# Attention with a gated MLP on one core: V straight from DRAM a period ahead, and the value product in three runs with MLP products between

## The chip, the cores and the metric

The kernel runs on one core of one Trainium2 chip. The metric is the device time of one execution in microseconds (us). It was run three times; the profile is of one more execution. TensorE is called PE here, VectorE DVE, ScalarE ACT, GpSimd POOL, and the queue of SyncE, which issues most DMAs, SP.

## The reference, cut to what matters

```python
def _attn_ref(q, k, v):                       # q, k, v: [8, 8, 576, 64] float32
    scores = (1 / sqrt(64)) * q @ k.T
    mask = pos[:, None] // 64 >= pos[None, :] // 64        # causal in blocks of 64
    scores = where(mask, scores, -1e9)
    attn = exp(scores - max(scores))
    attn = attn / (sum(attn) + 1e-9)
    return attn @ v

x = attn_out.transpose(0, 2, 1, 3).reshape(4608, 512)
gate = 1 / (1 + exp(-(x @ w_gate)))           # [512, 1536]
return gate * (x @ w_val) @ w_out             # [1536, 512]
```

The three weights come as 64-bit floats and are converted on the chip.

## The kernel before, in words

**Stages.** The attention takes the first half of the time. It runs over 32 head pairs p (8 batches of 4 pairs). Pairs 0 to 7 are done in one way and pairs 8 to 31 in another (`rest`), which is the one that the change touches. While the attention runs, PE is filled with products of the first third of the MLP (`mlp1`): 144 products of 128 x 512 for each batch, in groups that accumulate in two PSUM banks. The second half of the time is the other two thirds of the MLP (L1123, L1208), which the change leaves alone.

**One period of a late pair.** For pair p, PE computes the scores in three groups (`s`: query blocks 3, 2, and 1 with 0), then those of the last 64 queries of both heads (`t`, the tail). DVE masks them and takes the row maxima (L435, L486). ACT takes the exponentials (L443, L488). DVE then transposes the probabilities in blocks of 32 x 32 into the tile Z (L571 for the blocks, L579 and L582 for the tail). The order on DVE and on ACT is written out by hand (`line`): the tail's transposes come after those of blocks 3 and 2, and those of blocks 1 and 0 after the tail's. Then PE multiplies by V (`z_half`, all through the helper at L308): 144 float32 matmuls on 32 rows and 64 columns of the array, which stand in the trace as 288 records and as many weight loads. It comes in two parts. The first, at step `half`, takes the 10 key blocks that need Z from blocks 3, 2 and the tail (160 records). The second, at step `AV` of the next period, takes the other 8 (128 records). `z_out` (L609, L611) then copies the result, and the next pair's scores follow at once. `FX` multiplies by the reciprocal row sums, which go to DRAM (`r_d`) and come back broadcast (`rb`), splits the result for the MLP and stores it.

**Where MLP products go.** A period is a list of steps with a number of places ("ticks") behind each. For the late pairs the list is `REST`:

```python
REST = (("AV", 0), ("s", 3), ("t", 2), ("tr3", 1), ("tr2", 1), ("trt", 2), ("half", 0), ("trl", 1), ("k", 0), ("FX", 0), ("r", 1), ("q", 1))
```

That is 12 ticks. In each tick `rate` products are put into the order, 3 on the average in the steady state (36 in a period): 9 behind the scores, 18 between the tail's scores and `half`, 9 between the two parts of the value product. The order is held: `half` and `AV` stand behind the last 8 products put before them (`recent`), products put behind them stand behind their last matmul (`hold`), and the scores stand behind the last product. `KEEP` is the number of products that are left when a new batch's products come in.

**V.** One 32-row copy of V is loaded from DRAM for each head (L246, two DMAs of 144 KB), behind the load of the reciprocals on SP. Three more DMAs copy it to the other three groups of 32 partitions (L249, 288 KB each) and wait for the first two. The load for pair p + 1 is put at the end of period p. There are two buffers (`VR`, one of them a part of the tile ZV), so it can start when the value product of pair p - 1 is done. K and Q of pair p + 3 are loaded in steps `k` and `q` (L279, four DMAs each).

**DMA slots.** Every DMA of SP and ACT takes one of eight semaphores in turn, and a DMA waits on its queue until the one that had its semaphore before has landed.

Of the kernel before, what the change touches and what calls it, by code (L numbers as in the profile page):

```python
# [23 lines left out]
KEEP = (52, 32)  # L24
# [8 lines left out]
REST = (("AV", 0), ("s", 3), ("t", 2), ("tr3", 1), ("tr2", 1), ("trt", 2), ("half", 0), ("trl", 1), ("k", 0), ("FX", 0), ("r", 1), ("q", 1))  # L33
# [3 lines left out]
TICKS = 12  # L37
ZB, ZG, ZH = 480, 112, 1920
# [4 lines left out]
def attn_glu_kernel(ctx: ExitStack, tc: tile.TileContext, q, k, v, w_gate, w_val, w_out, out):  # L43
# [142 lines left out]
    with ExitStack() as s2:  # L186
# [53 lines left out]
        def load(p, what, queue=nc.sync):  # L240
            b, hp = pairs[p]
            h0 = 2 * hp
            if what == "v" and p > N_FIRST:
                VR = VRs[(p + 1) % 2]
                for h in range(2):
                    behind(nc.sync.dma_start(out=VR[0:32, h], in_=v[b, h0 + h].rearrange("(t p) d -> p t d", p=32)).ins,  # L246
                           loads["rb"])
                for a in range(1, 4):
                    dma = nc.sync.dma_start(out=VR[32 * a:32 * a + 32], in_=VR[0:32])  # L249
                loads["SP"] = dma.ins  # L250
                return
# [25 lines left out]
            for h in range(2):  # L277
                for j in range(2):
                    bulk(queue.dma_start(  # L279
                        out=r[64 * h + 32 * j:64 * h + 32 * j + 32].rearrange("p (t a) -> p t a", a=32),  # L280
                        in_=src[b, h0 + h, :, 32 * j:32 * j + 32].rearrange("(t p) a -> p t a", p=32)))

        pe_last, first_mm, hold, dealt, chain = [], [], [], [], []
        last, loads, q_copied, recent = {}, {}, [], []

# [21 lines left out]
        def matmul(*args, **kw):  # L307
            pe_last[:] = [nc.tensor.matmul(*args, **kw).ins]  # L308
            in_turn()

        def transpose(*args):
            pe_last[:] = [nc.tensor.transpose(*args).ins]
            if hold:
                behind(pe_last[0], hold[0])
            in_turn()
# [87 lines left out]
        def attend(p):  # L403
# [88 lines left out]
            def recip():  # L492
# [12 lines left out]
                if rest:  # L505
# [5 lines left out]
                    loads["rb"] = dma.ins  # L511
# [3 lines left out]
                loads["rb"] = dma.ins  # L515
# [70 lines left out]
            pv = []  # L586

            def z_half(second):
                if not pv:
                    pv.extend(two_banks() for _ in range(2))  # L590
                VR = VRs[(p + 1) % 2]
                for n, kb in enumerate((0, 4, 1, 5, 2, 6, 3, 7) if second else (8, 12, 9, 13, 10, 14, 11, 15, 16, 17)):
                    g = kb // 4
                    lo, z = (32 * g, ZB * (kb % 4) + (ZG + 32) * g) if g < 4 else (P, 2 * P + 16 * (kb % 4))
                    for a in range(4):
                        at_rows = slice(32 * a, 32 * a + 32)
                        for h in range(2):
                            first = n == 0 and not second
                            matmul(pv[a // 2][rows(h), a % 2, lo:144], lhsT=VR[at_rows, h, kb],
                                   rhs=Z[at_rows, ZH * h + z:ZH * h + z + 144 - lo], start=first,  # L600
                                   stop=(n == (7 if second else 9)), tile_position=(32 * a, 64 * h), skip_group_check=second)
                            if n == a == h == 0:
# [57 lines left out]
            def step(what):  # L660
# [20 lines left out]
                elif what == "half":  # L681
                    z_half(False)
# [8 lines left out]
                elif what == "warm":  # L691
                    if p == 1:
                        warm()
                elif what == "av":
                    if rest:
                        z_half(True)
# [286 lines left out]
        pe_ticks = []  # L983
# [72 lines left out]
        for p in range(n + 1):  # L1056
# [4 lines left out]
            for what, places in (ALONE if p < NP else FIRST if p < N_FIRST else TURN if p == N_FIRST else JOIN if p == N_FIRST + 1 else REST):  # L1061
                if what.startswith(("AV", "TR", "FX")):
                    if prev:
                        prev(what.lower() if what in ("AV", "FX") else what.lower()[:2] + what[2:])
                    if prev and what == "AV" and pairs[p - 1][1] == NP - 1:
# [3 lines left out]
                        rate = (left - KEEP[pb > 0]) / (4 * TICKS)  # L1069
# [7 lines left out]
                elif now:  # L1077
                    now(what)
                for _ in range(places if now else 6 if what == "AV" else 0):
                    pe_ticks.append(pe_last[0])  # L1080
                    acc += rate
                    while acc >= 1:
                        acc -= 1
                        left -= 1
                        ins = next(mlp, None)
# [14 lines left out]
            if N_FIRST <= p and p + 1 < n:  # L1100
                load(p + 1, "v")
# [268 lines left out]
```

## Time and profile before

| | us |
|---|---|
| runs of the kernel before (3): median | 1269.74 |
| lowest, highest | 1256.24, 1270.45 |
| the profiled execution: device time | 1269.53 |
| its span, first to last instruction | 1267.7 |
| PE busy | 1166.6 (92%) |
| DVE busy | 899.1 (71%) |
| ACT busy | 548.3 (43%) |
| POOL busy | 341.6 (27%) |
| mean granted TensorE clock, share of full speed | 0.95 |

A row of a timeline begins with the start and the length in us; "x160" counts the instructions that are merged in it; in brackets stands the idle time before the first of them and what ended it. "issue" means that nothing in the profile held the engine. SPq and ACTq are the queues' own rows. A busy PE is not a PE at full speed: the granted clock (PEclk, as a share) stands beside it.

### The profile page before, as it was taken

To read this page: it belongs to the slowest core of one execution; us is meant where nothing else is said; L and a number is where in the kernel's file an instruction comes from. 1 tells how busy PE (TensorE), PEld (TensorE's weight loads), DVE (VectorE), ACT (ScalarE), POOL (GpSimd) and SP (SyncE) were. 2 spreads that over 40 slices of the span, in tenths; PEclk is the share of its full clock that TensorE was granted. 3 is DMA by queue.
4 is the path that set the end of the run, shared out by engine and by line. 5 is a ranking of instruction groups with operands and counts; after the bars stand their busy time and mean duration, and the time that the engine had idled before them with its cause. 6 is when DMAs were issued, how large, how long until landed. Compare 5 with 4: busy or idle time off the path is not lost.

```text
span 1267.7 us, 30599 instructions
## 1 busy us (share of the span) xinstructions
PE 1166.6 (92%) x12073; PEld 941.5 (74%) x12073; DVE 899.1 (71%) x1844; ACT 548.3 (43%) x1274; POOL 341.6 (27%) x380
## 2 busy tenths in 40 slices
PE   8899789888889878888799999999999999999998
PEld 5566678666767666667577888888888888888887
DVE  5878567556565656565599795888999876768564
ACT  5876435344344434344324444454454532323222
POOL 3446323232231321322230110101111134251402
PEclk9999899888888888888899999999999999999999
DMA  6656555656566556564633314266386956253532
GB/s 162 171 142 152 120 122 116 143 110 144 113 127 137 122 113 136 118 133 111 174 102 109 124 50 133 47 181 164 69 216 242 310 182 211 90 183 104 162 112 72
DMA packets 314688, 175.32 MB, mean 138 GB/s; under 512 B 239152, under 2 KB 279088, under 8 KB 311600
## 3 DMA queue, kind: packets, MB, share of 16 engines
q1 hardware_dynamic: 303744, 154.84, 48.5%
q10 hardware_dynamic: 10416, 17.47, 3.8%
q8 instruction: 95, 1.56, 0.5%
q0 software_dynamic: 384, 1.05, 0.2%
q14 instruction: 49, 0.40, 0.1%
HBM read 104.73 MB, written 47.33 MB: 120 GB/s over the span
## 4 chain that ended last, share of the span: by engine, by line
PE 68%; DMA 11%; DVE 8%; SPq 5%; issue 3%; ACT 3%; POOL 1%; ACTq 0%; DVEq 0%
PE b L1123 26%; PE bank L308 11%; PE m L1208 8%; PE b L1208 8%; PE m L153 8%; PE m L160 4%; DMA VR<-VR 3%; PE bank L153 2%; DMA ZV<-ZV 2%; ACT P L443 2%; SPq L279 2%; DMA r_d<-rT 1%; DMA rb<-r_d 1%; DVE ZV L571 1%; DMA ZV<-in_v_dram 1%
## 5 line engine op out<-in xcount | busy, mean ns | idle before, releaser
L1123 PE MATMUL b<-XH,w 128*128 128x512 f32 (+1 forms) x1120 | 320.9, 368 | 0.8 <-ACT p L1141 0.5
L1123 PEld LDWEIGHTS b<-XH,w 128*128 128x128 f32 x1120 | 203.5, 188 | 37.6 <-ACT p L1141 0.8
L1123 PE MATMUL b<-XL,w 128*128 128x512 f32 (+1 forms) x560 | 205.6, 368 | 0.0
L443 ACT ACTIVATE P<-bank,nm 128x512 f32<-128x512 f32 (+3 forms) x256 | 132.1, 530 | 54.7 <-DVE nm L435 51.7
L1123 PEld LDWEIGHTS b<-XL,w 128*128 128x128 f32 x560 | 105.6, 189 | 17.6 <-DVE XL L958 0.2
L308 PE MATMUL bank<-ZV 32*64 32x48 f32 (+5 forms) x3680 | 83.8, 272 | 24.7 <-DMA ZV<-ZV 14.6
L955 ACT CAST XH<-XB 128x1024 fp32r<-128x1024 f32 (+1 forms) x72 | 66.9, 942 | 88.0 <-DVE XB L953 53.3
L435 DVE TENSOR_REDUCE nm<-bank 128x2 f32<-128x1024 f32 (+3 forms) x128 | 102.5, 821 | 3.1
L308 PEld LDWEIGHTS bank<-ZV 32*64 32x64 f32 (+1 forms) x3680 | 66.9, 142 | 47.7 <-DMA ZV<-ZV 16.9
L609 DVE COPY xT<-bank 128x256 f32<-128x256 f32 x24 | 10.2, 425 | 127.1 <-PE bank L308 127.1
L308 PE MATMUL bank<-ZV,VR 32*64 32x80 f32 (+4 forms) x3456 | 63.5, 275 | 36.6 <-DMA VR<-VR 27.2
L1208 PE MATMUL m<-wo,hH 128*128 128x512 f32 x288 | 93.2, 389 | 0.0
L308 PEld LDWEIGHTS bank<-ZV,VR 32*64 32x64 f32 x3456 | 55.8, 151 | 50.0 <-DMA VR<-VR 25.1
L1208 PE MATMUL b<-wo,hH 128*128 128x512 f32 x288 | 92.9, 389 | 0.0
L160 PE MATMUL m<-wo,hH 128*128 128x512 f32 x256 | 91.3, 427 | 1.6 <-ACT hH L177 1.6
L940 POOL TENSOR_TENSOR XB<-XB 128x256 f32<-128x256 f32 x30 | 23.9, 797 | 248.1 <-DMA XB<-xT_d 190.1
L958 DVE TENSOR_TENSOR XL<-XB,XH 128x1024 fp32r<-128x1024 f32 (+1 forms) x72 | 78.4, 1092 | 13.5 <-ACT XH L955 13.3
L153 PE MATMUL m<-XH,wg 128*128 128x512 f32 x240 | 87.3, 421 | 0.4 <-ACT t L170 0.4
L153 PE MATMUL m<-XH,wv 128*128 128x512 f32 x240 | 86.3, 417 | 0.1
L571 DVE STREAM_TRANSPOSE ZV<-P 128x512 f32<-128x512 f32 (+1 forms) x192 | 80.1, 474 | 0.0
L637 POOL TENSOR_TENSOR xT<-xT,rb 128x576 f32<-128x576 f32 x24 | 34.7, 1448 | 158.1 <-DMA rb<-r_d 53.9
L160 PEld LDWEIGHTS m<-wo,hH 128*128 128x128 f32 x256 | 53.2, 209 | 15.1 <-ACT hH L177 2.9
(214 smaller groups left out, 2467.5 us busy)
## 6 DMA issues: line engine op xcount, KB each, us to landing
XB<-xT_d SPq DMA_DIRECT2D x48, 256.0 KB
prr<-part_d SPq DMA_DIRECT2D x46, 256.0 KB
VR<-VR SPq DMA_DIRECT2D x36, 288.0 KB
ZV<-ZV SPq DMA_DIRECT2D x36, 288.0 KB
part_d<-ost SPq DMA_DIRECT2D x36, 256.0 KB
part_d<-ost ACTq DMA_DIRECT2D x32, 256.0 KB
xT_d<-xT ACTq DMA_DIRECT2D x28, 288.0 KB
rqk<-in_k_dram SPq DMA_DIRECT2D x108, 72.0 KB
```

The costliest lines, as they stand in the source:

```text
L153: mm = nc.tensor.matmul(ps, lhsT=lh, rhs=rh, start=(i == 0), stop=(i == n - 1))
L160: mm = nc.tensor.matmul(ps, lhsT=lh[:, f, t * P:(t + 1) * P], rhs=rh, start=(f == i == 0), stop=(f == F1 - 1 and i == 2))
L279: bulk(queue.dma_start(out=r[64 * h + 32 * j:64 * h + 32 * j + 32].rearrange("p (t a) -> p t a", a=32), in_=src[b, h0 + h, :, 32 * j:32 * ...
L308: pe_last[:] = [nc.tensor.matmul(*args, **kw).ins]
L435: line("DVE", nc.vector.tensor_reduce(out=nm[:, c0:c0 + 2], in_=ps[:, :, c:c + P * (i + 1)], axis=AX.X, op=ALU.max, negate=True), rest)
L443: line("ACT", nc.scalar.activation(out=Pi[:, h], in_=ps[:, h, c:c + n], func=AF.Exp, bias=nm[:, c0 + h:c0 + h + 1], accum_out=sm[:, 5 * h ...
L571: line("DVE", nc.vector.transpose(out=dst[:, :, :4 * ZG].rearrange("p b (g x) -> p b g x", g=4)[:, :, :i + 1, :32], in_=Pi[:, h].rearrange ...
L637: nc.gpsimd.tensor_mul(out=xT, in0=xT, in1=rb)
L955: cut = nc.scalar.copy(out=XO[j][0][:, a:b, c], in_=x)
L958: sub = nc.vector.tensor_sub(out=XO[j][1][:, a:b, c], in0=x, in1=XO[j][0][:, a:b, c].bitcast(F32))
L1123: mm = nc.tensor.matmul(ps, lhsT=lh, rhs=rh, start=(first and k == 0), stop=(k == n - 1), skip_group_check=not first)
L1208: mm = nc.tensor.matmul(po[t], lhsT=lh[:, f, t * P:(t + 1) * P], rhs=rh, start=(half == 0 and i == 0), stop=(half == 1 and i == 5))
```

## The change

V of pair p + 1 is loaded by eight DMAs straight from DRAM, one for each head and group of 32 partitions, at step `tr3` of period p, behind the last marked DMA of SP (`last["SPq"]`, the reciprocals' or the late pairs' K and Q). The value product takes its key blocks in another order (`KBS`) and in two or three runs, whose lengths `av_runs` chooses by a count of issued TensorE instructions. With three runs the next period follows the list `WIDE`: the second run and four ticks come ahead of `AV`. Of the products between the tail's scores and `half`, one tick is moved behind `half`. The rate is worked out again in each period.

```diff
-KEEP = (52, 32)
+KEEP = (52, 40)
-REST = (("AV", 0), ("s", 3), ("t", 2), ("tr3", 1), ("tr2", 1), ("trt", 2), ("half", 0), ("trl", 1), ...
+REST = (("AV", 0), ("s", 3), ("t", 2), ("tr3", 1), ("tr2", 1), ("trt", 1), ("half", 0), ("trl", 2), ...
+WIDE = (("AVa", 4), *REST)
+MEAN = 13.5
+KBS = (8, 12, 9, 13, 10, 14, 11, 16, 15, 0, 4, 1, 5, 2, 6, 3, 17, 7)
+FETCH, FETCH_AT, ROUND, APART, GAP = 256, 192, 32, 25, 24
...
-                for h in range(2):
-                    behind(nc.sync.dma_start(out=VR[0:32, h], in_=v[b, h0 + h].rearrange("(t p) d -> p t d", p=32)).ins,
-                           loads["rb"])
-                for a in range(1, 4):
-                    dma = nc.sync.dma_start(out=VR[32 * a:32 * a + 32], in_=VR[0:32])
+                for a in range(4):
+                    for h in range(2):
+                        dma = nc.sync.dma_start(out=VR[32 * a:32 * a + 32, h],
+                                                in_=v[b, h0 + h].rearrange("(t p) d -> p t d", p=32))
+                        behind(dma.ins, last["SPq"])
+                        last["SPq"] = dma.ins
...
+        def av_runs():
+            x = (FETCH_AT - issued[0]) % FETCH
+            def fits(runs):
+                spans, t = [], 0
+                for r in runs:
+                    spans.append((t, t + ROUND * r))
+                    t += ROUND * r + GAP
+                return all(sum(max(0, min(b, e + FETCH) - max(a, e)) for a, b in spans) <= FETCH - APART
+                           for e in range(x - FETCH, t, FETCH))
+            two = [(n, 18 - n) for n in (9, 10, 8, 11, 7)]
+            three = [(n, m, 18 - n - m) for n in (6, 7, 8, 9, 5, 4) for m in (6, 5, 7, 4, 3)]
+            return next((r for r in two + three if fits(r)), (6, 6, 6))
...
-            def z_half(second):
+            def z_run():
                 if not pv:
                     pv.extend(two_banks() for _ in range(2))
+                    lengths = av_runs()
+                    wide[:] = [len(lengths) > 2]
+                    kbs = list(enumerate(KBS))
+                    runs[:] = [[kbs.pop(0) for _ in range(r)] for r in lengths]
                 VR = VRs[(p + 1) % 2]
-                for n, kb in enumerate((0, 4, 1, 5, 2, 6, 3, 7) if second else (8, 12, 9, 13, 10, 14, 11, 15, 16, 17)):
+                kbs = runs.pop(0)
+                for n, kb in kbs:
...
+            steps = (ALONE if p < NP else FIRST if p < N_FIRST else TURN if p == N_FIRST else JOIN if p == N_FIRST + 1 else
+                     WIDE if wide[0] else REST)
+            ticks = sum(places for _, places in steps)
...
+                    if what == "tr3" and N_FIRST <= p and p + 1 < n:
+                        load(p + 1, "v")
+                new = what == "AV" and pairs[p - 1][1] == NP - 1
+                if p <= N_FIRST and new and p:
+                    rate = (left - KEEP[0]) / (4 * TICKS)
+                elif p > N_FIRST and (new or tick == 0):
+                    i, keep = (p % NP, KEEP[1]) if p % NP or new or p == N_FIRST + 1 else (NP - 1, 0)
+                    rate = max(0, left - keep) / (ticks - tick + (NP - 1 - i) * MEAN)
...
-            if N_FIRST <= p and p + 1 < n:
-                load(p + 1, "v")
```

## Rows read from the trace of the kernel before

**Rows 1.** Windows: late pairs' scores 9 to 31; second half. Length, busy, PEclk, DMA, GB/s.

```profile
core 0: us, PE busy (x) PEld busy (x) DVE busy (x) ACT busy (x) POOL busy (x), PEclk, DMA share, GB/s
146.46:622.34 475.88, 402.00 (x7783) 325.33 (x7778) 282.47 (x683) 197.18 (x575) 134.52 (x177) 0.87 0.58 126
...
660.00:1267.70 607.70, 601.24 (x2801) 502.33 (x2799) 476.46 (x889) 237.71 (x395) 125.82 (x114) 1.00 0.47 144
```

**Rows 2.** Waits of PE over the span: total us, times, longest us.

```profile
PE bank L308 <- DMA VR<-VR: 27.2, 20, 2.3
PE bank L308 <- DMA ZV<-ZV: 14.6, 11, 2.9
PE bank L308 <- issue: 13.8, 8, 4.2
PE bank L308 <- ACT xT L611: 10.3, 3, 4.2
PE m L160 <- POOL hL L178: 4.8, 2, 2.5
```

**Rows 3.** Timeline of PE, one period without a wait: scores, half, products, AV, scores.

```profile
428.44 0.49 PE L308 MATMUL bank<-KH,QH 64*128 64x512 f32 x2
...
437.66 1.99 PE L308 MATMUL bank<-ZV,VR 32*64 32x80 f32 x160
439.58 0.50 PE L153 MATMUL m<-XL,wv 128*128 128x512 f32 x1
...
441.85 2.17 PE L308 MATMUL bank<-ZV,VR 32*64 32x144 f32 x128
443.95 0.50 PE L308 MATMUL bank<-KH,QH 64*128 64x512 f32 x2
```

**Rows 4.** Windows from half to AV: without a wait; with a 1.70 us one; with 1.68.

```profile
437.66:441.92 4.26, 4.26 (x178) 3.58 (x180) 4.19 (x13) 1.76 (x3) 1.50 (x3) 1.00 0.27 68
393.89:402.98 9.09, 7.39 (x177) 5.95 (x180) 4.32 (x13) 2.35 (x4) 3.27 (x6) 0.62 0.68 159
...
479.86:486.31 6.45, 4.72 (x169) 3.72 (x169) 4.31 (x13) 2.35 (x4) 3.29 (x6) 1.00 0.82 203
```

**Rows 5.** Timeline of DVE: tail's transposes in three periods.

```profile
393.14 0.89 DVE L579 STREAM_TRANSPOSE ZV<-Pt 128x128 f32<-128x128 f32 x4 [0.52 <-ACT Pt L488]
...
413.11 0.89 DVE L579 STREAM_TRANSPOSE ZV<-Pt 128x128 f32<-128x128 f32 x4
...
436.79 0.85 DVE L579 STREAM_TRANSPOSE ZV<-Pt 128x128 f32<-128x128 f32 x4
```

**Rows 6.** Timeline of PE: scores that belong to the first two; half of pair 31.

```profile
384.54 0.49 PE L308 MATMUL bank<-KH,QH 64*128 64x512 f32 x2
...
405.02 0.50 PE L308 MATMUL bank<-KH,QH 64*128 64x512 f32 x2
...
634.20 0.40 PE L308 MATMUL bank<-ZV 32*64 32x80 f32 x16 [2.53 <-DVE ZV L579]
634.53 0.59 PE L153 MATMUL bank<-XH,wg 128*128 128x512 f32 x1
```

**Rows 7.** Timeline of PE: a wait of products between half and AV, and the AV after.

```profile
291.90 0.50 PE L160 MATMUL m<-wo,hH 128*128 128x512 f32 x1
...
295.89 0.50 PE L160 MATMUL m<-wo,hL 128*128 128x512 f32 x1 [2.35 <-POOL hL L178]
...
297.90 3.22 PE L308 MATMUL bank<-ZV 32*64 32x144 f32 x128
301.05 0.50 PE L308 MATMUL bank<-KH,QH 64*128 64x512 f32 x2
```

**Rows 8.** Timeline of SP's queue in the period of rows 3.

```profile
426.06 0.98 SPq L246 DMA_DIRECT2D VR<-in_v_dram  x2
430.15 1.99 SPq L249 DMA_DIRECT2D VR<-VR  x3
439.50 2.27 SPq L279 DMA_DIRECT2D rqk<-in_k_dram  x4
```

**Rows 9.** DMA of 426.0:430.15, then 430.15:435.5: packets, MB, share of 16 engines.

```profile
q1 hardware_dynamic: 2553, 0.45, 63.0%
...
q1 hardware_dynamic: 128, 0.88, 79.5%
```

**Rows 10.** Timeline of ACT and its queue around a late store.

```profile
491.21 0.34 ACTq L794 DMA_DIRECT2D part_d<-ost  x1
491.65 0.37 ACT L609 COPY xT<-bank 128x256 f32<-128x256 f32 x1 [5.54 <-DMA rb<-r_d]
```

More of the change, by code (lines that the diff above doesn't have):

```diff
@@ L278, in load @@
                 for j in range(2):
-                    bulk(queue.dma_start(
+                    dma = bulk(queue.dma_start(
                         out=r[64 * h + 32 * j:64 * h + 32 * j + 32].rearrange("p (t a) -> p t a", a=32),
                         in_=src[b, h0 + h, :, 32 * j:32 * j + 32].rearrange("(t p) a -> p t a", p=32)))
+                    if p > N_FIRST + 3:
+                        last["SPq"] = dma.ins
         pe_last, first_mm, hold, dealt, chain = [], [], [], [], []
         last, loads, q_copied, recent = {}, {}, [], []
+        issued = [0]
+        def av_runs():
[10 more added lines that the diff above has]
+            return next((r for r in two + three if fits(r)), (6, 6, 6))
         def mark(engine, ins):
@@ L308, in matmul @@
             pe_last[:] = [nc.tensor.matmul(*args, **kw).ins]
+            issued[0] += 4 if kw["lhsT"].dtype == F32 else 2
             in_turn()
@@ L312, in transpose @@
             pe_last[:] = [nc.tensor.transpose(*args).ins]
+            issued[0] += 2
             if hold:
@@ L510, in recip @@
                                                 in_=tails[:, h].partition_broadcast(D))
-                    loads["rb"] = dma.ins
+                    last["SPq"] = dma.ins
                     return
@@ L514, in recip @@
                     dma = nc.sync.dma_start(out=rb[rows(h), o:o + n], in_=r_f[f:f + n].partition_broadcast(D))
-                loads["rb"] = dma.ins
+                last["SPq"] = dma.ins
                 rb_last[:] = [dma.ins] if p < N_FIRST else []
@@ L597, in z_half @@
                         for h in range(2):
-                            first = n == 0 and not second
                             matmul(pv[a // 2][rows(h), a % 2, lo:144], lhsT=VR[at_rows, h, kb],
-                                   rhs=Z[at_rows, ZH * h + z:ZH * h + z + 144 - lo], start=first,
-                                   stop=(n == (7 if second else 9)), tile_position=(32 * a, 64 * h), skip_group_check=second)
-                            if n == a == h == 0:
+                                   rhs=Z[at_rows, ZH * h + z:ZH * h + z + 144 - lo], start=(n == 0),
+                                   stop=(kb == kbs[-1][1]), tile_position=(32 * a, 64 * h),
+                                   skip_group_check=(kbs[0][0] > 0))
+                            if kb == kbs[0][1] and a == h == 0:
                                 for ins in recent:
@@ L693, in step @@
                         warm()
+                elif what == "ava":
+                    z_run()
                 elif what == "av":
                     if rest:
-                        z_half(True)
+                        z_run()
                         z_out()
@@ L1084, in attn_glu_kernel @@
                         left -= 1
+                        issued[0] += 2
                         ins = next(mlp, None)
```

13 lines of the change are left out of this document (6 added, 7 removed).

## The prediction, made before the changed kernel was run

> **What bounds the kernel now.** First I read the windows of the two halves [rows 1]. In the second half PE is busy for 601.24 of 607.70 us at a granted clock of 1.00, and the change doesn't touch it. From the scores of pair 9 to those of pair 31, 22 periods, PE is idle for 73.9 of 475.88 us and the mean granted clock is 0.87. That stretch is what the change can win in, at 475.88 / 22 = 21.63 us a period. Then I read who PE waited for [rows 2]: V's copies, 27.2 + 14.6 us (VR and ZV are the two buffers), waits that no instruction explains ("issue"), 13.8 us, a copy of ACT, 10.3, and a lower half of the MLP's hidden values from POOL, 4.8. Then I looked for a period without waits, and there is one [rows 3]: scores at 428.44, half at 437.66, products at 439.58, AV at 441.85, the next scores at 443.95. It took 15.51 us. The other 6 us of the mean period are waits and what the clock does after them. The stretch from half to AV shows that best [rows 4]: 4.26 us without a wait, 9.09 with one wait of 1.70 us for V. Of the 4.83 us more only 1.70 are the wait; the other 3.13 are instructions at a lower clock (0.62 granted in the mean; of the two levels, 1.2 and 2.4 GHz, the lower stood for most of it). So a wait of PE is paid about twice or more, when it brings the clock down.
>
> Last I looked at what stands just behind V. In the period without waits the tail's last transposes on DVE run from 436.79 to 437.64 [rows 5], and half starts at 437.66 [rows 3]. From the scores' start to the end of these transposes it takes 9.20 us here, and in two other periods 414.00 - 405.02 = 8.98 and 394.03 - 384.54 = 9.49 [rows 5, 6]. It is a chain of reductions, exponentials and transposes that PE can't shorten, and half needs its end. With 27 products between scores and half, PE arrives at the same moment: the old order is balanced against DVE, and V's lateness hides how tightly.
>
> **The change part by part.**
>
> *V.* Before, two loads are issued from 426.06 and the copies at 430.15 [rows 8], when both have landed; half wants them at 437.66. When the load gets through later they come too late: 31 waits, 41.8 us [rows 2]. After, the load stands a whole period ahead of its use, behind a buffer that is free when AV of the pair before it is done. I take V's waits to go entirely. What it costs on the DMA engines: the three copies took 79.5% of 5.35 us, 4.3 us of 16 engines [rows 9]; the window of the two loads, in which K and Q packets run too, has 2553 small packets at 63% of 4.15 us, or 1.0 us for each 1000. V has 1152 rows of 256 bytes in one copy, so 4608 packets in the new form: 4.7 us against 4.3 + 1.2 = 5.5 before. That is about equal, so with the DMA engines 58% busy [rows 1] I cost it at nothing. On SP's queue eight issues at about 0.49 us (0.98 for two) take 3.9 us instead of 0.98 + 1.99. They stand where SP now waits for the first loads to land, before K's loads at 439.50 [rows 8], a hole of over 7 us after the copies; K, the reciprocals and Q behind them aren't later. The bounds for V are 0 and, if it came as late as now, 41.8 / 22 = 1.9 us a period.
>
> *The runs.* Worked through, `av_runs` never finds two runs: over two runs with a gap of 24 some block of 256 lies inside them and holds 232 or more of their instructions, and 231 are allowed. So it is three runs of about six key blocks, and `WIDE` with 16 ticks, from pair 9 on. Its rate is then near 36 / 16 = 2.25 products a tick (2.5 for a batch's first pair, 1.8 for its last). Between scores and half stand 8 ticks instead of 9, at the lower rate: about 18 products instead of 27. Nine products take 2.27 us (439.58 to 441.85) [rows 3], so PE arrives at half 9.22 - 2.27 = 6.95 us after the scores, while DVE still ends at about 9.2. A new wait of 2.2 us a period takes the place of V's, bounded by 1.5 (20 products, chain 9.0) and 3.1 (14 or 15 products, chain 9.5). It exists already where the last pair's half waited 2.53 us for L579 [rows 6].
>
> From half to the next scores the value product needs 1.92 + 2.10 = 4.02 us as now [rows 3], and two gaps of 9 products, 4.54 us: 8.6 us. A period at full clock is so 9.2 + 8.6 = 17.8 us. This is longer than the 15.51 of the undisturbed period, and shorter than the mean of 21.63.
>
> *The clock.* After a wait of 2.35 us for POOL the next AV took 3.22 us instead of 2.17, and all from 291.90 to 301.05 [rows 7] took 9.15 us where ten products and AV need 4.6 and the waits 2.5 (a short one of ACT among them): some 2.0 us lost. The 1.70 us wait lost 3.13 us; one of 1.68 us lost nothing, its window has a granted clock of 1.00 [rows 4]. So a wait of the new length lowers the clock in some periods and not in others: bounds 0 and 3.1 us a period. I take two of three, at 2.5 us: 1.7 us.
>
> *Instruction stalls.* The "issue" waits stand at L308, the line of the value product and the scores, up to 4.2 us each [rows 2]. With gaps of products in every block of 256 they should mostly go; bounds 0 and 13.8 / 22 = 0.6 us a period, I take 0 here. The Trainium skill says otherwise (Runtime: NRT & Kernel Launch, Instruction fetch mechanics): instructions are refilled in blocks of 256, and the crossing is mostly hidden behind the pace of issue, so that the third run would buy nothing. The trace of before disagrees, with eight such waits of 13.8 us in all; no run here has shown yet that they go with the third run. By that rule, what the waits are would remain, and the sum below would be 1240.
>
> *Other waits.* The copies of ACT and the values from POOL cost (10.3 + 4.8) / 22 = 0.7 us a period now [rows 2]. Some of it falls before half and is covered by DVE's chain: I take 0.2.
>
> The sum is 17.8 + 1.7 + 0.2 = 19.7 us a period, 1.93 less than 21.63; over 22 periods 42.5 us. Against the profiled execution, 1269.5 us with a span of 1267.7 (the median of the runs shown is 1269.74, the same for this purpose), that makes 1227 us. PE's products aren't fewer, only placed differently, so the second half starts that much earlier and takes as long as before.
>
> **The rivals.**
>
> *A, the clock holds.* The wait for DVE stands between products and short runs of six key blocks instead of ten, and the wait of 1.68 us left the clock alone [rows 4]. For it: less light work follows each wait. Against it: 2.35 us brought the clock down [rows 7]. The period is then 17.8 + 0.2 = 18.0 us: 80 us won, 1190.
>
> *B, the clock falls in every period.* The new wait is longer than V's single waits and comes in all 22 periods, V's only in some. The period is 17.8 + 3.1 + 0.4 = 21.3 us, 1262: the gain is given back. For it stand the 3.13 us of [rows 4]; against it the window with 1.00.
>
> *C, slower: ACT held by a store.* ACT works in order, and a store on its queue may have to wait for the DMA that had its slot. At 491.21 a store of a finished part went out only when a load of the reciprocals had landed, and ACT had been idle for 5.54 us [rows 10]; PE's longest wait for such a copy was 4.2 us [rows 2]. Eight V loads in a row take all eight slots. A store placed behind them holds the exponentials, so the chain to half, until V has landed. Such a period costs 19.7 + 4.2 and the rest of the clock's full price, 1.4: 25.3 us. If it strikes in a share x of the periods, the mean is 19.7 + 5.6 x. It breaks even with 21.63 at x = 0.34, and at x = 0.75 the time is 1227 + 22 x 4.2 = 1319. Against it: the loads can go out early in the period, and few waits of that kind show now.
>
> *D, V is late all the same,* because it queues on SP behind K, Q and the reciprocals: 1.9 us of wait beyond DVE's and the rest of the clock's price, 1.4, so 23.0 us and 1300 at worst; half of it, 1263, is likelier. The free buffer and a lead of a whole period speak against it.
>
> **How the numbers follow.** Forecast 0.52 (1205 to 1244), A 0.18, B 0.15, C 0.10, D 0.05. A measurement of this kernel can tell about 2% from no change, that is 1244 to 1295. Faster: forecast and A, 0.70. Same: B and D, 0.20. Slower: C, 0.10. The predicted time is 1227. The range goes from 1187, where A ends, to 1262, which takes in B; it leaves out C, D's worse part and a clock that never falls with a shorter chain.
>
> **What would show it.** If right, the profile after has no wait of PE for V; its new first wait is for DVE's L579 at each half, about 2 us, 20 times or more; the scores' pitch is 19 to 20 us; the granted clock of the stretch is near 0.9; the issue waits have all but gone. The wait for L579 being under 1 us would show my count of products, or the chain's 9.2 us, wrong. A granted clock of 1.00 with 2 us waits would prove A. A wait for ACT or for V's DMA in many periods would prove C or D. If no wait has gone, the forecast is wrong as a whole.

## The result, and the profile after

The changed kernel takes 1215.68 us (median of 4 runs, 1210.44 to 1219.20), the kernel before 1269.17 us beside it. The ratio is 0.9597, with a 95% interval from 0.9525 to 0.9669: faster, by 53.5 us where 42.5 were forecast. The profiled execution took 1219.2 us with a span of 1217.4. In the lines below the old L308 is L332, L571 is L597, L579 is L605, L609 and L611 are L640 and L642, L160 and L178 are L164 and L182, and L246 is L251.

The page's busy times and clock, 40 slices of the span:

```profile
PE 1143.8 (94%) x12073; PEld 914.0 (75%) x12073; DVE 905.3 (74%) x1844; ACT 547.6 (45%) x1274; POOL 340.2 (28%) x380
...
PEclk9999999999989989999899999999999999999999
DMA  7667897897887878796323232545587845344432
```

The waits of PE, as [rows 2]:

```profile
PE bank L332 <- DVE ZV L605: 20.6, 15, 3.7
PE bank L332 <- issue: 20.2, 20, 3.9
PE bank L332 <- ACT t L174: 6.5, 5, 1.3
```

No wait for V is left. In its place stands DVE's L605, the tail's transposes. The five waits named ACT t are the wait of `half` too, and so is the one named ACT Pt (1.6 us). Two of the fifteen lie outside the 22 periods, the 3.7 us one among them. Inside them `half` waits in 19 periods, 0.97 to 1.57 us each, 24.7 us in all and 1.30 in the mean; the first three periods, with 20 to 26 products ahead of `half`, have no such wait over 0.3 us. The third thing to see is the second line: the "issue" waits haven't gone. Their sum is 20.2 us where it was 13.8, but it is a mixed one. Sorted by place (as under "Runs placed by the counted stream"), ten such waits, 13.3 us with one of L164, longest 3.9, are of the kind that made up all eight, 13.8 us, before. One of 2.8 us stands ahead of scores 9, and the others, 0.74 us at most, mostly at the tail's scores and at `half`. So the stalls of the old kind are as large as before.

The windows, as [rows 1]: the 22 periods from scores 9 to scores 31, one of them alone, and the second half:

```profile
148.93:570.43 421.50, 376.85 (x7781) 295.92 (x7777) 283.86 (x683) 195.98 (x574) 133.90 (x177) 0.98 0.83 141
226.05:244.61 18.56, 16.96 (x359) 13.35 (x354) 13.46 (x32) 9.35 (x27) 6.00 (x8) 1.00 0.81 138
660.00:1217.40 557.40, 552.11 (x2587) 462.29 (x2585) 438.36 (x807) 217.18 (x365) 125.68 (x114) 1.00 0.48 148
```

A period takes 421.50 / 22 = 19.16 us instead of 21.63, at a granted clock of 0.98 instead of 0.87. That is 54.4 us over 22 periods. Scores 9 start 2.5 us later than before, and from scores 31 to the end it takes 1.6 us longer (1217.40 - 570.43 against 1267.70 - 622.34): 50.3 us in all between the two profiled executions. The periods had lengths from 15.51 to 26.55 us before; now 20 of 22 lie between 17.4 and 20.2, and two have 23.59 and 24.24.

The timeline of PE for the period of the second window, cut to the scores, the tail's scores, the last product before `half`, the three runs with the products at their ends, and the next scores:

```profile
226.05 0.50 PE L332 MATMUL bank<-KH,QH 64*128 64x512 f32 x2
...
230.13 0.40 PE L332 MATMUL bank<-KH,QBH 128*128 128x288 f32 x1 [0.20 <-ACT P L469]
...
233.57 0.39 PE L157 MATMUL m<-XL,wg 128*128 128x512 f32 x1
235.35 1.34 PE L332 MATMUL bank<-ZV 32*64 32x80 f32 x96 [1.40 <-DVE ZV L605]
236.62 0.73 PE L157 MATMUL m<-XH,wg 128*128 128x512 f32 x2
...
239.11 1.72 PE L332 MATMUL bank<-ZV 32*64 32x80 f32 x96
240.76 0.50 PE L157 MATMUL m<-XH,wv 128*128 128x512 f32 x1
...
243.03 1.65 PE L332 MATMUL bank<-ZV 32*64 32x112 f32 x96
244.61 0.50 PE L332 MATMUL bank<-KH,QH 64*128 64x512 f32 x2
```

Three runs of six key blocks (96 records each), as worked out. On DVE the four transposes that `half` waits for end at 235.49, 9.44 us after the scores' start, where [rows 5, 6] had 8.98 to 9.49; `half` itself starts at 235.35. PE stands ready at 233.96, 7.91 us after the scores' start:

```profile
234.62 0.87 DVE L605 STREAM_TRANSPOSE ZV<-Pt 128x128 f32<-128x128 f32 x4
```

One of the two long periods has this in the timeline of PE: the run that begins at 344.90 stands still for 3.43 us before its last record, and nothing in the profile holds it:

```profile
342.98 0.40 PE L164 MATMUL m<-wo,hH 128*128 128x512 f32 x1
344.90 1.32 PE L332 MATMUL bank<-ZV 32*64 32x80 f32 x95 [1.52 <-DVE ZV L605]
349.65 0.23 PE L332 MATMUL bank<-ZV 32*64 32x48 f32 x1 [3.43 <-issue]
```

### The profile page after: what moved, and what is told of

The parts are those of the page before. It is cut to its first block, busy times and chain, and to the rows that moved or that the text cites. A ratio compares the mean times of both kernels' runs of the same rounds, so it can differ in the third digit from the quotient of the medians.

```text
span 1217.4 us, 30724 instructions
## 1 busy us (share of the span) xinstructions
PE 1143.8 (94%) x12073; PEld 914.0 (75%) x12073; DVE 905.3 (74%) x1844; ACT 547.6 (45%) x1274; POOL 340.2 (28%) x380
## 4 chain that ended last, share of the span: by engine, by line
PE 66%; DVE 10%; DMA 8%; ACT 6%; issue 5%; SPq 4%; POOL 1%; ACTq 0%; DVEq 0%; POOLq 0%
PE b L1165 27%; PE bank L332 12%; PE m L1250 7%; PE b L1250 7%; PE m L157 7%; PE m L164 4%; ACT P L469 4%; DMA ZV<-in_v_dram 2%; DMA VR<-in_v_dram 2%; DMA r_d<-rT 2%; SPq L284 1%; PE bank L157 1%; DVE nm L461 1%; DMA XB<-xT_d 1%; DVE ZV L597 1%
## 5 line engine op out<-in xcount | busy, mean ns | idle before, releaser
L469 ACT ACTIVATE P<-bank,nm 128x512 f32<-128x512 f32 (+3 forms) x256 | 132.4, 535 | 54.7 <-DVE nm L461 52.4
L332 PE MATMUL bank<-ZV 32*64 32x48 f32 (+5 forms) x3680 | 82.5, 266 | 27.1 <-DVE ZV L605 14.9
L332 PEld LDWEIGHTS bank<-ZV 32*64 32x64 f32 (+1 forms) x3680 | 64.0, 137 | 48.8 <-DVE ZV L605 19.1
L164 PE MATMUL m<-wo,hH 128*128 128x512 f32 x256 | 88.9, 412 | 1.2 <-issue 0.7
L640 DVE COPY xT<-bank 128x256 f32<-128x256 f32 x24 | 10.2, 425 | 102.2 <-PE bank L332 102.2
L597 DVE STREAM_TRANSPOSE ZV<-P 128x512 f32<-128x512 f32 (+1 forms) x192 | 80.4, 476 | 0.0
L332 PE MATMUL bank<-ZV,VR 32*64 32x80 f32 (+4 forms) x3456 | 56.8, 255 | 17.7 <-ACT t L174 6.5
L332 PEld LDWEIGHTS bank<-ZV,VR 32*64 32x64 f32 x3456 | 48.7, 132 | 32.2 <-issue 14.3
L1250 PEld LDWEIGHTS b<-wo,hH 128*128 128x128 f32 x288 | 54.1, 188 | 11.2
```

The source lines that it names most:

```text
L164: mm = nc.tensor.matmul(ps, lhsT=lh[:, f, t * P:(t + 1) * P], rhs=rh, start=(f == i == 0), stop=(f == F1 - 1 and i == 2))
L469: line("ACT", nc.scalar.activation(out=Pi[:, h], in_=ps[:, h, c:c + n], func=AF.Exp, bias=nm[:, c0 + h:c0 + h + 1], accum_out=sm[:, 5 * h ...
L597: line("DVE", nc.vector.transpose(out=dst[:, :, :4 * ZG].rearrange("p b (g x) -> p b g x", g=4)[:, :, :i + 1, :32], in_=Pi[:, h].rearrange ...
L1250: mm = nc.tensor.matmul(po[t], lhsT=lh[:, f, t * P:(t + 1) * P], rhs=rh, start=(half == 0 and i == 0), stop=(half == 1 and i == 5))
```

## The experiments

Each run's ratio is to the kernel before, run on the same chip beside it. "Issue" in the text is PE's wait at the value product and the scores that no instruction explains.

**V alone, and the runs alone.** First the change was taken apart. e1 is the kernel before with nothing changed but V's loads:

```diff
-                for h in range(2):
-                    behind(nc.sync.dma_start(out=VR[0:32, h], ...
-                for a in range(1, 4):
-                    dma = nc.sync.dma_start(out=VR[32 * a:32 * a + 32], in_=VR[0:32])
+                for a in range(4):
+                    for h in range(2):
+                        dma = nc.sync.dma_start(out=VR[32 * a:32 * a + 32, h], ...
...
+                    if what == "tr3" and N_FIRST <= p and p + 1 < n:
+                        load(p + 1, "v")
```

> The kernel before with V's new loads alone (eight from DRAM, at step tr3, a period ahead); two runs, REST, KEEP and rate as before. Theory (V is the gain, the third run takes products away from in front of half and so makes the wait for DVE): V's waits go, 27 products stand before half again, the period is 15.5 us plus about 1 of issue waits, 0.7 of others and 0.5 of clock, 17.7 us: 1183 us, faster than the changed kernel's 1216, with waits for the tail's transposes under 5 us in all. Rival (runs of 320 and 256 instructions stall at the refill of instructions, and the clock falls with them): issue waits over 40 us, over 12 stretches of lower clock, a period over 20 us: 1235 or more.

e2 is the changed kernel with this diff turned round (two loads and three copies, at the end of the period):

> The changed kernel with V's old loads (two from DRAM, three copies, at the end of the period). Theory (the gain is V's): V's copies land about 9 to 11 us after the scores, as before, so half waits for V again, about 1 us beyond DVE's chain, and the clock falls in more periods: 20 to 20.5 us a period, 1235 to 1245. Rival (the runs and the products between them are the gain, since they keep the clock): near 1216 with V's waits under 10 us.

e1 took 1217.54 us, ratio 0.9642 [0.9599, 0.9685]; e2 1272.73 us, 1.0069 [1.0033, 1.0104]. The waits of PE in e1:

```profile
PE bank L311 <- issue: 25.5, 12, 4.9
PE bank L311 <- ACT xT L614: 9.5, 4, 3.0
PE m L160 <- POOL hL L178: 8.8, 4, 2.5
```

and in e2:

```profile
PE bank L331 <- DVE ZV L604: 25.4, 15, 9.0
PE bank L331 <- DMA ZV<-ZV: 22.1, 23, 1.7
...
PE bank L331 <- issue: 4.8, 9, 0.9
```

So the whole measurable gain is V's new loads. The runs alone gain nothing: V's old copies still arrive late (22.1 us, and 2.6 for VR), and the waits of `half` for DVE's chain come on top. e2's forecast of 1235 to 1245 missed. With V early, the runs change the form of the time and hardly its amount: the intervals of e1 and of the changed kernel overlap. e1 pays 18.3 us for ACT's copies and POOL's lower halves, which are 0.6 and 0.5 us in the changed kernel, and has no wait at `half`. Both theories for e1 missed: the time lies between them, since stalls came (25.5 us of issue, up to 4.9) but fewer than the rival's 40 us. e1's periods go from 15.50 to 24.11 us, in its second half mostly one of about 15.6 and one of 22 to 23.5 in turn. Of the eleven over 20 us four hold a wait of 2.3 to 3.0 us for POOL or for ACT's copy, and seven an issue stall of 1.7 to 4.9 us inside a run, as here:

```profile
214.92 1.90 PE L311 MATMUL bank<-ZV,VR 32*64 32x80 f32 x151
221.69 0.41 PE L311 MATMUL bank<-ZV,VR 32*64 32x16 f32 x9 [4.87 <-issue]
```

After such waits the clock falls: 14 stretches at the lower level between 145 and 640 us, against 17 in the kernel before and 5 in the changed one. Of the 13 inside e1's 22 periods seven follow an issue stall, three a copy of ACT and three POOL.

**Two runs instead of three.** e3 is the changed kernel with runs of ten and eight key blocks in the old order:

```diff
-MEAN = 13.5
-KBS = (8, 12, 9, 13, 10, 14, 11, 16, 15, 0, 4, 1, 5, 2, 6, 3, 17, 7)
+MEAN = 12
+KBS = (8, 12, 9, 13, 10, 14, 11, 15, 16, 17, 0, 4, 1, 5, 2, 6, 3, 7)
...
-            return next((r for r in two + three if fits(r)), (6, 6, 6))
+            return (10, 8)
...
-                elif p > N_FIRST and (new or tick == 0):
+                elif p > N_FIRST and (new or what == steps[0][0]):
```

> The changed kernel with two runs of 10 and 8 key blocks in the old order of blocks, the list REST (12 ticks, 3 products each), 24 products before half, 12 between the runs. Theory: the wait for the tail's transposes falls from 1.3 to about 0.6 us a period, issue waits are at most 25 us, the period is about 17.7: 1185. Rival (issue stalls and the clock in long runs): 1230 or more, issue waits over 40 us.

1230.47 us, 0.9734 [0.9698, 0.9771]: slower than the changed kernel. DVE's wait has shrunk to 2.2 us, but issue is 30.2 us in 14 waits, up to 4.9, and the clock fell 14 times. The theory's 1185 missed; the rival's time came, its 40 us of issue didn't. So short runs are worth something in the changed kernel's order; e1, with the same lengths as e3, did better by 13 us, and what the difference is (its list of steps, its rates) was not taken apart.

**Fewer packets for V.** e4 is the changed kernel with V as two loads and three copies again, but early:

```diff
-                for a in range(4):
-                    for h in range(2):
-                        dma = nc.sync.dma_start(out=VR[32 * a:32 * a + 32, h], ...
+                for h in range(2):
+                    dma = nc.sync.dma_start(out=VR[0:32, h], ...
+                    behind(dma.ins, last["SPq"])
+                    last["SPq"] = dma.ins
+                for a in range(1, 4):
+                    dma = nc.sync.dma_start(out=VR[32 * a:32 * a + 32], in_=VR[0:32])
```

> The changed kernel with V by two loads and three copies, but at tr3 a period ahead. Theory (the 256-byte packets fill the DMA engines, 0.83 of the stretch against 0.58, and slow the refill of instructions): the DMA share falls to about 0.65, issue waits from 20 to under 12 us, no wait for V; 1205 to 1210. Rival (the DMA engines have room, only the earlier load counts): the same within 3 us, 1213 to 1219, issue waits near 20 us.

1231.90 us, 0.9755 [0.9705, 0.9806]. Both expected times missed. The DMA engines are less busy (0.63 against 0.83 in the 22 periods), and yet it is slower, with 11 stretches of low clock and these issue waits:

```profile
PE bank L334 <- issue: 19.2, 19, 2.8
```

The busy share alone doesn't say what the stalls cost, and neither does the number of packets.

**More and fewer products ahead of `half`.** Is DVE's wait really the products that the change moved behind `half`? e5 moves two ticks back, from the gaps:

```diff
-REST = (... ("trt", 1), ("half", 0), ("trl", 2), ...
-WIDE = (("AVa", 4), *REST)
+REST = (... ("trt", 3), ("half", 0), ("trl", 1), ...
+WIDE = (("AVa", 3), *REST)
-MEAN = 13.5
+MEAN = 16
```

> The changed kernel with two ticks of products moved back in front of half and one taken from each gap of a value product's runs (22 or 23 products before half instead of 18, gaps of about 7 instead of 9 or 10). Theory (the wait for the tail's transposes is the products that were moved away): that wait falls from 1.3 to about 0.4 us a period, under 10 us in all; with shorter gaps the issue waits rise by 0.2 to 0.4 us a period; 1203 to 1210. Rival (the wait is DVE's whatever stands before half, or the shorter gaps stall as long runs do): 1216 or more, with the wait for the transposes near 20 us or the issue waits over 30.

e6 moves two more out, so that 13 or 14 products stand before `half`:

```diff
-REST = (... ("tr2", 1), ("trt", 1), ("half", 0), ("trl", 2), ...
-WIDE = (("AVa", 4), *REST)
+REST = (... ("tr2", 0), ("trt", 0), ("half", 0), ("trl", 3), ...
+WIDE = (("AVa", 5), *REST)
-MEAN = 13.5
+MEAN = 16
```

> The changed kernel with one more tick of products in each gap and two fewer before half (13 or 14 before half, gaps of 11 or 12). Theory: the wait for the tail's transposes grows by what is taken away, about 1.1 us a period, to 45 us or more in all (ACT's part of the same wait with it); the issue waits of 0.6 to 0.9 us inside the second run go, those left stand at the tail's scores; the clock falls oftener; 1240 to 1250. Rival (gaps of 12 products are what the refill wants, and their price is hidden): 1205 to 1216.

e5: 1222.01 us, 0.9643 [0.9577, 0.9710]. e6: 1255.50 us, 0.9926 [0.9898, 0.9953]. The waits of PE in e5:

```profile
PE bank L332 <- issue: 19.9, 26, 2.9
PE m L164 <- POOL hL L182: 8.8, 5, 2.2
PE bank L332 <- DVE ZV L605: 5.8, 5, 4.7
```

and in e6, where the wait of `half` has another name, the exponentials of the tail just ahead of the transposes:

```profile
PE bank L332 <- ACT Pt L514: 42.6, 19, 2.6
PE bank L332 <- issue: 10.9, 11, 4.8
```

The wait follows the count of products. Summed at `half` over the 22 periods, whatever its name, it is 1.1 us in e5 (mostly 22 or 23 products; its 4.7 us wait lies outside), 25.7 in the changed kernel and 48.1 in e6, while `half` starts 8.7 to 9.5 us after the scores in nearly all of them. In e6 the wait is 2.2 us in the mean, the size that was forecast for the change, and there the clock does fall: 20 stretches, a mean of 0.92, 20.61 us a period. Its time is 5.5 us above its theory's range, and its rival is out. e5 shows the other side: DVE's wait gone, nothing won. Its time is in its rival's range (1216 or more), with neither of that rival's signs. POOL's lower halves (8.8 us) and stalls of 1.2 to 2.2 us came up behind it.

**Runs placed by the counted stream.** In the 22 late periods every issue stall of a microsecond or more in the traces of before, after, e1, e3 and e4 stands at one place of PE's stream: counting two instructions for each matmul, and the semaphore instructions on PE's queue, the count modulo 256 is 192 or 193. The kernel's own count, `issued`, leaves out the semaphore instructions, 5.3 a period in the changed kernel's trace, so its blocks drift. e7 puts them in, as 4.85 a period, and lets two runs in again where they fit:

```diff
-FETCH, FETCH_AT, ROUND, APART, GAP = 256, 192, 32, 25, 24
+FETCH, FETCH_AT, ROUND, APART, GAP = 256, 192, 32, 24, 24
...
-            x = (FETCH_AT - issued[0]) % FETCH
+            x = (FETCH_AT - issued[0] - 53 - 97 * (p - 8) // 20) % FETCH
...
-                elif p > N_FIRST and (new or tick == 0):
+                elif p > N_FIRST and (new or what == steps[0][0]):
```

> The changed kernel with its count mended: a gap of 24 instructions is enough in a block of 256 (APART 24), the semaphore instructions on TensorE's queue are counted in (53 and 4.85 a period), and the rate is worked out once a period. Two runs (9, 9) with 12 ticks then come in about half of the periods, (6, 6, 6) in the others. Theory (refill stalls come where a block lies inside a run, and two runs are as good where none does): periods of 16.5 to 17 and of 18.5 us, issue waits no more than 25 us and few over 2 us: 1190 to 1205. Rival (stalls come with any long run, wherever the block's edge is): issue waits over 30 us, 1220 or more.

1218.96 us, 0.9639 [0.9576, 0.9701]: no gain, a miss. Two runs came in 10 of the 22 periods, about as meant. Issue stayed at 20.3 us in 17 waits, up to 4.2; ACT's copies cost 7.6 us. Knowing the place wasn't enough to keep the stalls away.

**Less traffic for V.** e8 is e1, and e11 the changed kernel, each with only the first two of V's eight loads from pair 10 on; in the other three groups of partitions V stays that of an earlier pair, so three quarters of V are not loaded:

```diff
-                for a in range(4):
+                for a in range(4 if p < N_FIRST + 3 else 1):
```

> V's new loads alone in the kernel before (as e1_v_only), with only the first two of the eight loads from pair 10 on, so that three quarters of V are stale. Theory (V's packets delay the refill of instructions, which waits among them): issue waits fall from 25.5 to under 15 us, none over 3 us, the lower clock stands in fewer than 12 stretches; 1190 to 1200. Rival (the refill takes its 3.5 to 4 us by itself, V's traffic or not): issue waits 20 us or more, 1212 to 1222.

> The changed kernel with only the first two of V's eight loads from pair 10 on; three quarters of V are stale. Theory (V's packets are no free load: they delay the refills): the issue waits fall from 20.2 to about 10 (the tail's scores wait for a bank, not for a refill), none over 1 us, the lower clock stands in at most 3 stretches between 150 and 575 us; 1204 to 1210. Rival (V's packets cost nothing, as the prediction had it): 1213 to 1219, issue waits of 2 us and more still there.

e8: 1204.84 us, 0.9511 [0.9453, 0.9569]. e11: 1200.20 us, 0.9517 [0.9488, 0.9546]. The waits of PE in e8:

```profile
PE bank L311 <- ACT xT L614: 12.5, 5, 3.5
PE bank L311 <- issue: 10.2, 10, 1.8
PE m L160 <- POOL hL L178: 9.8, 4, 2.5
```

and in e11, with its 22 periods as a window:

```profile
PE bank L332 <- DVE ZV L605: 20.4, 15, 3.7
PE bank L332 <- ACT t L174: 6.5, 5, 1.3
...
PE bank L332 <- issue: 4.6, 9, 0.7
```

```profile
151.38:551.45 400.07, 367.67 (x7782) 290.20 (x7778) 283.88 (x683) 195.93 (x574) 134.05 (x177) 1.00 0.45 100
```

V's traffic delays the stream: with three quarters of it away issue falls from 25.5 to 10.2 us in the one pair and from 20.2 to 4.6 in the other, and the longest stall from 4.9 to 1.8 and from 3.9 to 0.7. At the place modulo 256 the changed kernel has 13.3 us and e11 none. Between these two the waits at `half` (DVE's and ACT t) are the same to 0.2 us; among the small ones POOL's and DVE's lower halves grew from 0.5 to 3.1 us. A period goes from 19.16 to 400.07 / 22 = 18.18 us; the medians differ by 15.5 us, but the intervals of the two ratios still touch. Those of e1 and e8 don't; there the medians differ by 12.7 us. The times lie 5 us above e8's forecast and 4 us below e11's. About half of the 21.4 us over 22 periods is the two long periods, which have 18.90 and 17.62 us here instead of 23.59 and 24.24.

**V in two parts, and POOL's share to DVE.** e9 is e5 with V's last four loads behind K's loads and the lower halves hL of the last hidden group of each batch (`f == F1 - 1`) on DVE instead of POOL; e10 is e1 with the same two edits; e12 is e5 with the second alone:

```diff
+                    if what == "k" and N_FIRST < p and p + 1 < n:
+                        load(p + 1, "v", parts=range(2, 4))
...
-                        load(p + 1, "v")
+                        load(p + 1, "v", parts=range(4 if p == N_FIRST else 2))
...
-                glu(mp, pg, pv, (hH[:, f], hL[:, f]), NM, nc.vector if b >= B - 1 else nc.gpsimd)
+                glu(mp, pg, pv, (hH[:, f], hL[:, f]), NM, nc.vector if b >= B - 1 or f == F1 - 1 else nc.gpsimd)
```

> As e5_more_ahead, with V's last four loads moved behind K's loads (step k) and the lower half of the last hidden block (f = 3) on DVE instead of POOL. Theory (its 1222 us are refills that wait among V's packets and products that wait for POOL, with the clock each brings down): waits for POOL's hL go from 8.8 to under 3 us, issue waits from 19.9 to about 14; 1195 to 1208. Rival (what is taken away is late elsewhere, in DVE's chain or ACT's stores): 1215 or more.

> As e1_v_only (two runs, old ticks) with the same two edits as e9. Theory: hL's 8.8 us go, issue waits fall from 25.5 to 15 to 18; those of ACT's copies (9.5) stay; the alternation of 15.5 us periods with 22 us ones loses some of the long ones; 1195 to 1208. Rival: the long periods stay, with other waits in them; 1215 or more.

> As e5_more_ahead, with the lower half of the last hidden block on DVE instead of POOL, and V's eight loads in one place as in the changed kernel. Theory (e9's loss was V's second place, ahead of the reciprocals, and hL's move is good): no more than 2 waits for ACT's copies, 4 us or less; hL's wait falls from 8.8 to under 3 us; issue waits near 20; 1200 to 1212, ahead of the changed kernel. Rival (the products that no longer wait for POOL meet the next wait at once): 1213 to 1225.

e9: 1237.56 us, 0.9809 [0.9776, 0.9842]. e10: 1237.06 us, 0.9804 [0.9770, 0.9837]. Both lose some 15 to 20 us against e5 and e1. PE's waits in e9 begin so:

```profile
PE bank L332 <- ACT xT L642: 27.6, 10, 4.3
PE bank L332 <- issue: 14.7, 24, 2.6
```

ACT's own waits in e9 say what held those copies:

```profile
ACT xT L640 <- DMA rqk<-in_q_dram: 49.6, 9, 6.7
```

and in the changed kernel the same line reads:

```profile
ACT xT L640 <- DMA rqk<-in_q_dram: 6.0, 2, 3.0
```

The copy itself needs nothing of Q: what waits is a store ahead of it on ACT's queue, for the DMA that had its slot. All nine waits have such a store just ahead of the copy, as the longest shows:

```profile
309.03 0.34 ACTq L827 DMA_DIRECT2D part_d<-ost  x1
309.40 0.37 ACT L640 COPY xT<-bank 128x256 f32<-128x256 f32 x1 [6.71 <-DMA rqk<-in_q_dram]
```

SP's queue in e9 shows four loads of V between K's and the reciprocals' store, which in the changed kernel follows K directly:

```profile
321.96 2.04 SPq L284 DMA_DIRECT2D rqk<-in_k_dram  x4
324.11 3.05 SPq L251 DMA_DIRECT2D VR<-in_v_dram  x4
327.25 1.44 SPq L529 DMA_DIRECT2D r_d<-rT  x4
328.87 1.24 SPq L284 DMA_DIRECT2D rqk<-in_q_dram  x2
```

All that follows is late by those 3 us, and the store waits for it. e12 leaves V where the change put it: 1213.90 us, 0.9616 [0.9581, 0.9652]. The copies' waits are gone, but issue is 29.7 us in 37 waits. So V's second place was e9's loss. e12 can't be told from the changed kernel (0.9597). Its time lies at the lower end of the rival's 1213 to 1225, and what the theory said of ACT's copies and of POOL came, but not the gain. No version tried that loads all of V beats the change measurably.

## Why the prediction was right, point by point

The direction, the mechanism and, within 12 us, the size were right: 1215.68 in a range of 1187 to 1262, 11.3 us below the 1227. The period was forecast at 19.7 us and is 19.16. Its terms, however, were not all right: the period at full clock was taken 0.8 us too short and the clock's price more than 1 us too high. That these errors cancel in part is luck.

**V.** Its waits went entirely, as said. e1 and e2 show that this edit is necessary and by itself sufficient for the gain that can be measured.

**V's cost on the DMA engines, "nothing".** This step failed. I compared the work of the engines, 4.7 against 5.5 us a period, and called it equal. The real share rose from 0.58 to 0.83, and the row of the data queue for the 22 periods shows why; before:

```profile
q1 hardware_dynamic: 145433, 46.14, 50.0%
```

and after:

```profile
q1 hardware_dynamic: 218809, 45.71, 73.0%
```

The bytes are nearly the same, the packets 1.5 times as many. From the single packets of the trace, those of 256 bytes, nearly all of them V's, took 31.1 ns in the mean, 20.9 before, where my price of 1.0 us for each 1000 is 16 ns. That makes 9.0 us of 16 engines a period, against 6.0 for the old loads and copies. My price came from a window in which the engines were idle for a third, and fell short where they are busier. By e11 three quarters of this traffic cost 15.5 us between medians (21.4 in the windows), by e8 12.7. That it is the packets' number is not shown: e4 has V's packets down to a quarter at the same place, and 19.2 us of issue. What the runs show is V's traffic at its new place in the period.

**The runs and the wait for DVE.** Three runs always, as worked out, and a wait of `half` for DVE's chain in 19 of the 22 periods, 20 or more having been forecast. Its size was put at 2.2 us and is 1.30 in the mean of 19 periods, below my lower bound of 1.5. DVE's chain was right (9.44 against 9.2 us). PE's arrival was not: 7.91 us after the scores instead of 6.95, because 19 products stand there instead of 18, and because the tail's scores now wait for a bank that ACT has not read yet (the [0.20 <-ACT P L469] of the timeline above): seven products and these scores take 2.99 us (228.04 to 231.03), as long as nine and the scores before (430.45 to 433.46, 3.01). With fewer products ahead of them they come too early, which I didn't look at. My upper bound of 3.1 us was also worked out wrong: with 14 or 15 products by the same rows PE arrives at about 6.1 us, and 9.5 - 6.1 is 3.4.

**From `half` to the next scores.** 8.6 us forecast, 9.26 measured (244.61 - 235.35). The three runs take 1.27 + 1.65 + 1.58 = 4.50 us from start to the next product's start, where two took 4.02, and the gaps of ten and nine products 4.76 instead of 4.54. So the period at full clock is 18.56 us where 17.8 was said.

**The clock.** 1.7 us a period, from two periods of three, was too much. With the full-clock period 18.56 (the 19 periods in which the clock held have 18.62 in the mean) only 19.16 - 18.56 = 0.6 us is left for clock, stalls and all the rest. The clock fell in 3 of the 22 periods, not in 15. Rival A, in which it holds, was so nearer on this term, and its time of 1190 was wrong for the other terms. What sets the two cases apart is the length of the wait, as far as the runs show. In e6 the clock fell in 19 of the 20 periods with a wait of 2.02 to 2.64 us at `half`, and in neither of the two with 1.69 and 1.74. In the changed kernel, with 1.57 at most, it fell three times, twice of them after an issue stall of 3.4 or 3.9 us. That is rival B's mechanism, with its condition not met. The length of one wait isn't all: in e2 the clock fell in 12 periods without a wait over 1.67 us, and in ten of these two to five waits come close together. And the window of the 1.68 us wait, which I read as losing nothing, is 6.45 - 4.26 - 1.68 = 0.5 us longer, at a granted clock of 1.00.

**"The issue waits all but gone."** Wrong: 20.2 us. The stalls that the term meant are 13.3 us of them, 0.6 us a period where I took 0 and had 0.6 as the upper bound. They did shorten with the runs where V's traffic is small or later in the period: 4.8 us and at most 0.9 in e2, 4.6 and 0.7 in e11. With all of V's traffic at the new place they came back. The rule that I set against my 0, in the Trainium skill (Runtime: NRT & Kernel Launch, Instruction fetch mechanics), is that instructions are refilled in blocks of 256 and the crossing is mostly hidden. The traces bear out the blocks: the stalls stand at one place modulo 256. They don't bear out that it is always hidden, the longest single stalls being 2.8 to 4.9 us in the five traces of before, after, e1, e3 and e4; that the third run buys nothing holds for the time of e1 against the change, but not for its parts (stalls at the place 25.9 against 13.3 us, longest 4.9 against 3.9, low clock 14 times against 5).

**Rivals C and D.** D didn't come: no wait for V. C's mechanism, ACT's store held by its slot's DMA, is real, but not where the change puts V: ACT's waits for such DMAs are 6.8 us after (6.0 for Q's load and 0.8 for the reciprocals') against 19.6 + 4.0 + 0.8 before. It struck in e9 and e10, where V's loads stand ahead of the reciprocals: 49.6 us on ACT, 27.6 on PE.

Left open: why e7's placing of the runs brought nothing, why e3 is slower than e1, and what V with less traffic, but all of it loaded, would bring; that last was not tried.

## What to carry to other kernels

Before an early load is called free, look at what else uses the DMA engines where it will stand: here 9.0 us of their time a period went in where 6.0 had been, and the one to pay was PE, whose instructions come by DMA too (the row "q8 instruction" below). A price per packet from a window with idle engines falls short in a busy one. When a wait is taken away, look at the next thing that ends at the same moment (here DVE's chain to `half`), and weigh the wait that comes instead by its length and its neighbours: here single waits of 1.0 to 1.6 us by themselves left the clock alone in all but one period, and those of 2.0 to 2.6 brought it down in 19 of 20. A wait named "issue" is worth locating by its place in the engine's instruction stream before it is put down to noise.

## What the runs showed of the hardware that was not expected

**Where issue stalls stand, and when they end.** In the late periods all long ones have the same place modulo 256 in PE's stream, and each of 2 us or more in these five traces ends 1.2 to 1.6 us after a 16 KB packet of the instruction queue q8 has landed. By this count PE has 24,333 instructions, which are 95 blocks of 256, and q8 has 95 packets. In the changed kernel the packet runs from 346.76 to 348.30 us and PE goes on at 349.65; in e1 from 218.92 to 220.17 and 221.69. The DMA view of 343 to 349.7 us in the changed kernel shows that packet among V's and K's:

```profile
q1 hardware_dynamic: 3437, 0.78, 101.8%
q10 hardware_dynamic: 75, 0.17, 8.5%
q8 instruction: 1, 0.02, 1.4%
...
VR<-in_v_dram SPq DMA_DIRECT2D x3, 144.0 KB
rqk<-in_k_dram SPq DMA_DIRECT2D x4, 72.0 KB
```

That the late packet is the cause of the stall is the reading that fits all of them, and e8 and e11 agree with it; no run delayed that packet alone. In a run of the value product PE uses up instructions fastest: 95 records, 190 instructions, in 1.32 us above. All eight stalls of the kernel before follow a block with 240 or more instructions of the value product. In the changed kernel, with products between the runs, the six stalls behind blocks with 232 or more come to 4.3 us, 0.9 at most. But its two long ones follow blocks with only 190 and 170, which took 8.8 and 9.9 us: there the packet was late although PE was slow. With three quarters of V away, in e11, none of the 62 blocks ends in a stall.

**Large packets are no remedy.** In e4 V's copies go in packets of 9216 bytes, which take about 730 ns each by the trace. Its long stalls are still 2.05 to 2.8 us, with the DMA engines at 0.63. In e2, with the same copies later in the period and a share of 0.58, the longest is 0.9. So the size of the packets alone doesn't set the stalls; whether their place in the period or the share does was not separated. The share itself is a sum of packet times, which can overlap: in the view above it comes to more than 100%.
